# A layer norm's factors, worked out for four token tiles at once, in the last stage of a Fourier, expert and SoLU kernel

## The chip, the cores and the metric

The kernel runs on one core of a Trainium2 chip. The metric is device time in microseconds (us). Before the change three runs took 2077.13, 2080.64 and 2082.59 us; the median is 2080.64. The engines of a core are named PE (TensorE, matrix products), DVE (VectorE), ACT (ScalarE), POOL (GpSimd) and SP (SyncE, which here issues the transfers).

## The reference, cut to what matters

The reference is a chain of three parts: a two-dimensional Fourier transform of 8 x 3072 x 256 numbers, a layer of eight experts in which each of the 24,576 tokens goes to one expert at most, and a gated layer with a layer norm. The change lies in the third:

```
h = x @ w_in                          # 256 -> 1024
e = exp(h - max(h))
sm = e / (sum(e) + 1e-9)
solu = h * sm
mu, var = mean(solu), mean((solu - mu) ** 2)
ln = (solu - mu) / sqrt(var + 1e-6) * g_ln
out = ln @ w_out                      # 1024 -> 256
```

Everything is per token (a row). A layer norm takes out any factor of its row, except that the small 1e-6 has to be scaled with it. The kernel uses that: it never divides by sum(e). It forms u = c * h * e, with some factor c for the row, multiplies u by the weights (the mean is taken out of the weights beforehand), and scales the row of the result by a factor worked out from the sum of e, the variance of u, and c.

## The kernel before, in words

The program runs the Fourier stage, the experts, and then the last stage, which takes the second half of the span. The last stage works on 192 tiles of 128 tokens. Its order is written out by hand: a short list of steps for the first six tiles (`FILL`), and then a loop in which step t does the following, each engine taking its own instructions in this order.

- `mm1(t)`: twelve products on PE give `h` in PSUM, 128 tokens by 1024 (L989). Three buffers of `h`.
- `softmax(t)`: VectorE takes the negative maximum of the row (L999) and scales it (L1000). L1002 makes a power of two out of the maximum's exponent. POOL bounds it (L1003) and multiplies it by the token's input scale (L1004): that is c, one number per token. ScalarE takes the exponential, with the row's sum (L1007).
- `xsplit(t + 7)`: the inputs come in groups of four tiles. With the group's first tile VectorE takes the largest absolute value and makes four small columns of scales `v` (L925 to L929), and POOL multiplies the inputs by one of them (L934); with the second ScalarE rounds them to 16 bits (L945); with the third POOL takes the remainder (L947). The step that has a group's first tile is a step t with t = 1 modulo 4.
- `solu(t - 1)`: VectorE forms u = h * c * e with its sum (L1015). This is the last reader of `h`. ScalarE rounds u to 16 bits (L1018) and takes the sum of squares around the mean (L1020).
- `split(t - 2)`: VectorE takes the remainder (L1026), SP issues a transpose of both halves (L1029), and POOL works out the row's factor in six small instructions of one column (L1031 to L1036; L1035 is the power of -0.5).
- `mm2(t - 5)`: 24 products on PE (L1044 to L1046) into `po`, of which there are two buffers; ScalarE scales the rows by the factor and frees `po` (L1049); the result goes out through SP (L1055) for even tiles, and through a POOL transfer with a list of rows (L1058) for odd ones.

The small per-token columns of a tile lie in `s`, ten columns, with eight buffers. `half` holds -0.5 for the power; `gi`, `wgi` and `wgs` are scales of the weights.

Of the kernel before, what the change touches and what calls it, by code (L numbers as in the profile page):

```python
# [7 lines left out]
FP32 = mybir.dt.float32  # L8
# [3 lines left out]
I32 = mybir.dt.int32  # L12
U32 = mybir.dt.uint32
ACTF = mybir.ActivationFunctionType
ALU = mybir.AluOpType
# [7 lines left out]
F = 1024  # L23
# [26 lines left out]
HEAD_AT = 8  # L50
LAGS = [(2, 4, 5, 2)] * 5 + [(2, 3, 4, 4)] * 2 + [(2, 3, 4, 12)]
WARM = 18
STEPS = [[6, 6]] * 8


@with_exitstack
def kernel(
# [25 lines left out]
    nc = tc.nc  # L83
# [6 lines left out]
    keep = ctx.enter_context(tc.tile_pool(name="keep", bufs=1))  # L90
# [3 lines left out]
    gi = keep.tile([128, 1], FP32, name="gi")  # L94
    gsi = keep.tile([128, 1], FP32, name="gsi")
    wgi = keep.tile([128, 1], FP32, name="wgi")
    wgs = keep.tile([128, 1], FP32, name="wgs")
    half = keep.tile([128, 1], FP32, name="half")
    sc1 = keep.tile([128, 2, E], FP32, name="sc1")
    sc2 = keep.tile([128, 2, E], FP32, name="sc2")  # L100
    ke = keep.tile([128, E], FP32, name="ke")
# [5 lines left out]
    def pow2(dst, src, floor, factor):  # L107
        nc.vector.tensor_scalar(out=dst.bitcast(I32), in0=src.bitcast(I32), scalar1=0x7F800000, scalar2=None, op0=ALU.bitwise_and)
        nc.vector.tensor_scalar(out=dst, in0=dst, scalar1=floor, scalar2=factor, op0=ALU.max, op1=ALU.mult)
# [101 lines left out]
    with ExitStack() as fctx:  # L211
# [128 lines left out]
        groups = [0]  # L340
# [196 lines left out]
        warm = ps2.tile([128, 2, 147], FP32, name="s2")  # L537
        for _ in range(WARM):
            nc.tensor.matmul(warm.rearrange("p a b -> p (a b)"), junk[:, 0:128], junk[:, 0:294], start=True, stop=True)
# [59 lines left out]
        for b in range(B):  # L599
# [15 lines left out]
            ends, k = {}, 0  # L615
            for n in STEPS[b]:
                ends[k + n - 1] = (k, n)
# [264 lines left out]
    with ExitStack() as sctx:  # L882
        XB = 4
        NT = N // 128
        FIRST_X = [1, 1, 2, 2, 2]
        groups = FIRST_X + [XB] * ((NT - sum(FIRST_X)) // XB)
        where = [(g, i) for g, n in enumerate(groups) for i in range(n)]
# [12 lines left out]
        stp = sctx.enter_context(tc.tile_pool(name="sst", bufs=8))  # L900
        op = sctx.enter_context(tc.tile_pool(name="so", bufs=3))
        psh = sctx.enter_context(tc.tile_pool(name="psh2", bufs=3, space=PSUM))
        pso = sctx.enter_context(tc.tile_pool(name="pso", bufs=2, space=PSUM))
        st = {}
        odd = vp.tile([128, B * 12], I32, name="odd", bufs=1)
        nc.sync.dma_start(out=odd, in_=c_out)

        def own_out(r, mine, others):
# [13 lines left out]
        def xscale(g):  # L922
            n = groups[g]
            v = vp.tile([128, 4, XB], FP32, name="v")[:, :, 0:n]
            nc.vector.tensor_reduce(out=v[:, 0], in_=st["x", g], axis=AX.X, op=ALU.max, apply_absolute_value=True)  # L925
            pow2(v[:, 0], v[:, 0], 2.0 ** -100, 0.25)
            nc.vector.reciprocal(v[:, 1], v[:, 0])
            nc.vector.tensor_scalar(out=v[:, 2], in0=v[:, 0], scalar1=wgi, scalar2=None, op0=ALU.mult)
            nc.vector.tensor_scalar(out=v[:, 3], in0=v[:, 0], scalar1=wgi, scalar2=2.0 ** 12, op0=ALU.mult, op1=ALU.mult)  # L929
            st["v", g] = v  # L930
            st["x16", g] = x16p.tile([128, 2 * XB * D], FP16, name="x16")[:, 0:2 * n * D].rearrange("p (s j d) -> p s j d", s=2, d=D)
            if g >= POOL_X:
                r = v[:, 1].unsqueeze(2).to_broadcast([128, n, D])
                nc.gpsimd.tensor_tensor(out=st["x", g], in0=st["x", g], in1=r, op=ALU.mult)  # L934
# [57 lines left out]
        def softmax(t):  # L992
            if t >= NT:
                return
            (g, i), h = where[t], st["h", t]
            v = st["v", g][:, 2, i:i + 1]
            s = stp.tile([128, 10], FP32, name="s")
            st["s", t] = s
            nc.vector.tensor_reduce(out=s[:, 0:1], in_=h, axis=AX.X, op=ALU.max, negate=True)  # L999
            nc.vector.tensor_scalar(out=s[:, 0:1], in0=s[:, 0:1], scalar1=v, scalar2=None, op0=ALU.mult)  # L1000
            si = s.bitcast(I32)
            nc.vector.tensor_scalar(out=si[:, 1:2], in0=si[:, 0:1], scalar1=0x7F800000, scalar2=0x7F800000, op0=ALU.bitwise_and, op1=ALU.bitwise_xor)  # L1002
            nc.gpsimd.tensor_scalar(out=si[:, 1:2], in0=si[:, 1:2], scalar1=0x40000000, scalar2=None, op0=ALU.min)  # L1003
            nc.gpsimd.tensor_scalar(out=s[:, 8:9], in0=s[:, 1:2], scalar1=st["v", g][:, 3, i:i + 1], scalar2=None, op0=ALU.mult)  # L1004
            e = ep.tile([128, F], FP32, name="e")
            st["e", t] = e
            nc.scalar.activation(out=e, in_=h, func=ACTF.Exp, bias=s[:, 0:1], scale=v, accum_out=s[:, 3:4])  # L1007

        def solu(t):
            if not 0 <= t < NT:  # L1010
                return
            h, e, s = st.pop(("h", t)), st.pop(("e", t)), st["s", t]
            u = up.tile([128, F], FP32, name="u")
            st["u", t] = u
            nc.vector.scalar_tensor_tensor(out=u, in0=h, scalar=s[:, 8:9], in1=e, op0=ALU.mult, op1=ALU.mult, accum_out=s[:, 4:5])  # L1015
            u16 = u16p.tile([128, 2, F], FP16, name="u16")
            st["u16", t] = u16
            nc.scalar.copy(u16[:, 0], u)  # L1018
            j = jp.tile([128, F], BF16, name="j")
            nc.scalar.activation(out=j, in_=u, func=ACTF.Square, bias=s[:, 4:5], scale=-float(F), accum_out=s[:, 5:6])  # L1020

        def split(t):
            if not 0 <= t < NT:
                return
            u, u16, s = st.pop(("u", t)), st.pop(("u16", t)), st["s", t]
            nc.vector.tensor_tensor(out=u16[:, 1], in0=u, in1=u16[:, 0], op=ALU.subtract)  # L1026
            ut = utp.tile([128, 16, 128], FP16, name="ut")
            st["ut", t] = ut
            nc.sync.dma_start_transpose(out=ut, in_=u16.rearrange("p a f -> p (a f)"))  # L1029
            q = s[:, 6:7]  # L1030
            nc.gpsimd.tensor_scalar(out=s[:, 2:3], in0=s[:, 1:2], scalar1=2.0 ** 12, scalar2=None, op0=ALU.mult)  # L1031
            nc.gpsimd.tensor_scalar(out=q, in0=s[:, 3:4], scalar1=1e-9, scalar2=s[:, 2:3], op0=ALU.add, op1=ALU.mult)  # L1032
            nc.gpsimd.tensor_scalar(out=q, in0=q, scalar1=q, scalar2=1e-6, op0=ALU.mult, op1=ALU.mult)  # L1033
            nc.gpsimd.tensor_scalar(out=s[:, 5:6], in0=s[:, 5:6], scalar1=float(F) ** -3, scalar2=q, op0=ALU.mult, op1=ALU.add)  # L1034
            nc.gpsimd.tensor_tensor(out=s[:, 7:8], in0=s[:, 5:6], in1=half, op=ALU.pow)  # L1035
            nc.gpsimd.tensor_scalar(out=s[:, 7:8], in0=s[:, 7:8], scalar1=gi, scalar2=None, op0=ALU.mult)  # L1036

        def mm2(t):
            if not 0 <= t < NT:
                return  # L1040
            ut = st.pop(("ut", t))
            po = pso.tile([128, D], FP32, name="po")
            for k in range(8):
                nc.tensor.matmul(po, ut[:, k], wk["gg"][:, k, 0], start=k == 0, stop=False)  # L1044
                nc.tensor.matmul(po, ut[:, k], wk["gg"][:, k, 1], start=False, stop=False)  # L1045
                nc.tensor.matmul(po, ut[:, 8 + k], wk["gg"][:, k, 0], start=False, stop=k == 7)  # L1046
            s = st.pop(("s", t))
            o = op.tile([128, D], FP32, name="o")
            nc.scalar.activation(out=o, in_=po, func=ACTF.Copy, scale=s[:, 7:8])  # L1049
            b, j = divmod(t // 2, 12)  # L1050
            k1 = 4 * j + 1

            def put(lo, hi, tok, steps):
                dst = bass.AP(tensor=out.tensor, offset=out.offset + (b * S + tok) * D, ap=[[n * D, c] for n, c in steps] + [[1, D]])
                own_out(nc.sync.dma_start(out=dst, in_=o[lo:hi]), "even", ("odd",))  # L1055

            if t % 2:
                r = nc.gpsimd.indirect_dma_start(  # L1058
                    out=out,
                    out_offset=bass.IndirectOffsetOnAxis(ap=odd.bitcast(U32)[:, t // 2:t // 2 + 1], axis=0),  # L1060
                    in_=o,
                    in_offset=None,
                    bounds_check=N - 1,
                    oob_is_err=False,
                )
                own_out(r, "odd", ("even", "odd"))
            elif j < 11:
                put(0, 128, k1, [(1, 4), (96, 32)])
            else:
                put(0, 96, k1, [(1, 3), (96, 32)])  # L1070
                put(96, 112, 0, [(96, 16)])
                put(112, 128, 48, [(96, 16)])

        with tc.manual_schedule():
# [8 lines left out]
            for t in range(FILLED, NT + LAG + 1):  # L1083
# [3 lines left out]
                g = xsplit(t + AHEAD)  # L1087
# [121 lines left out]
```

## Time and profile before

| | |
|---|---|
| time, three runs | 2077.13, 2080.64, 2082.59 us |
| span of the profiled execution | 2072.3 us |
| time of the profiled execution | not given beside its span |
| granted TensorE clock, mean over the span | 0.983 |
| busy share of the span | PE 92%, PEld 70%, DVE 79%, ACT 70%, POOL 71% |
| chain that ended last, largest shares | POOL 35%, issue 13%, ACT 3%, DVE 2% |
| first and last start of L989 (the last stage) | 971.6 and 2040.6 us |

The profile is one execution of the program; its times count from the start of its span. "Busy" is the time in which an engine executes; register, branch, semaphore and transfer-issuing instructions don't count. A wait is put down to the instruction whose semaphore came last. Matrix products are pipelined, so the duration of a single one overlaps the next; the distance between starts is what counts. L numbers are lines of the kernel.

### The profile page before, as it was taken

The numbers are of one execution on the slowest core, as the hardware profiler recorded it, in microseconds if no ns is written. First come the engines' busy times: TensorE is split into PE (matmuls) and PEld (weight loads), VectorE is DVE, ScalarE is ACT, GpSimd is POOL, SyncE is SP. The second block draws the span as 40 slices with busy tenths as digits, with TensorE's granted clock in tenths as the row PEclk, the third lists the DMA queues.
The fourth block names the chain that finished last, engine by engine and source line by source line (L and its number), as shares of the span: only waits on it lengthen the run. The fifth ranks groups of instructions, "written<-read, shape, count | busy, mean of one in ns | idle before, by whom it ended". The sixth has DMA issues, their size and how long they took to land.

```text
span 2072.3 us, 43563 instructions
## 1 busy us (share of the span) xinstructions
PE 1912.2 (92%) x14621; PEld 1448.2 (70%) x14621; DVE 1646.0 (79%) x3426; ACT 1454.8 (70%) x2651; POOL 1463.0 (71%) x2260
## 2 busy tenths in 40 slices
PE   8999998789999999898999998999999999999997
PEld 7888886677878878786566665666666666666665
DVE  4767665688988889896988888888888888888884
ACT  6878875566667766684777776777777777677775
POOL 0455657776664566642888888888888888888886
PEclk9999999999999999999999999999999999999999
DMA  9776888233332333323878877888887788787775
GB/s 269 200 204 179 231 247 214 34 94 83 75 80 68 74 77 87 70 68 65 173 160 173 163 158 154 176 157 160 173 164 158 166 169 160 159 174 157 158 157 120
DMA packets 678311, 300.82 MB, mean 145 GB/s; under 512 B 580707, under 2 KB 658155, under 8 KB 678085
## 3 DMA queue, kind: packets, MB, share of 16 engines
q1 hardware_dynamic: 656981, 259.15, 58.4%
q0 software_dynamic: 20992, 38.84, 6.7%
q8 instruction: 115, 1.88, 0.4%
q14 instruction: 111, 0.91, 0.1%
q10 hardware_dynamic: 112, 0.04, 0.0%
HBM read 93.90 MB, written 65.95 MB: 77 GB/s over the span
## 4 chain that ended last, share of the span: by engine, by line
POOL 35%; issue 13%; ACT 3%; DVE 2%; PE 0%; POOLq 0%; DMA 0%; SPq 0%; ACTq 0%
POOL s L1031 5%; POOL out L1058 5%; POOL x L947 5%; POOL sx_sb L934 4%; POOL s L1035 4%; ACT j L1020 3%; POOL s L1004 3%; POOL s L1003 2%; POOL s L1032 2%; POOL s L1033 2%; POOL s L1034 2%; POOL s L1036 2%; DVE u L1015 1%; DVE s L999 0%; DVE u L1026 0%
## 5 line engine op out<-in xcount | busy, mean ns | idle before, releaser
L989 PE MATMUL h<-wi,xT 128*128 128x512 f16 x2304 | 530.5, 380 | 38.1 <-DVE u L1015 31.0
L1044 PE MATMUL po<-gg,ut 128*128 128x256 f16 x1536 | 419.2, 273 | 33.3 <-ACT o L1049 29.1
L989 PEld LDWEIGHTS <-xT 128*128 128x128 f16 x2304 | 221.3, 98 | 285.0 <-DVE u L1015 41.7
L1046 PE MATMUL po<-gg,ut 128*128 128x256 f16 x1536 | 419.2, 273 | 0.0
L1045 PE MATMUL po<-gg,ut 128*128 128x256 f16 x1536 | 419.2, 273 | 0.0
L1015 DVE SCALAR_TENSOR_TENSOR u<-h,s,e 128x1024 f32<-128x1024 f32 x192 | 246.2, 1282 | 164.2 <-POOL s L1004 164.1
L1018 ACT CAST u<-u 128x1024 f16<-128x1024 f32 x192 | 200.4, 1044 | 198.0 <-DVE u L1015 197.9
L453 POOL DMA_INDIRECT tab<-ent,r_ids x192 | 201.0, 1047 | 172.2 <-DMA xs<-t 67.7
L1026 DVE TENSOR_TENSOR u<-u,u 128x1024 f16<-128x1024 f32 x192 | 287.5, 1498 | 0.1
L1007 ACT ACTIVATE e<-h,s,v 128x1024 f32<-128x1024 f32 x192 | 230.4, 1200 | 45.0 <-DVE s L1000 36.6
L792 PE MATMUL py<-w2c,ht 128*128 128x256 f16 x832 | 229.1, 275 | 21.9 <-DVE ht L780 21.9
L773 PE MATMUL ph<-xT,w1c 128*128 128x256 f16 x832 | 227.6, 274 | 17.8 <-DMA xT<-x 13.8
L790 PE MATMUL py<-w2c,ht 128*128 128x256 f16 x832 | 229.1, 275 | 9.9 <-ACT ht L779 8.4
L999 DVE TENSOR_REDUCE s<-h 128x1 f32<-128x1024 f32 x192 | 232.7, 1212 | 0.7 <-PE h L989 0.7
L791 PE MATMUL py<-w2c,ht 128*128 128x256 f16 x832 | 228.9, 275 | 0.5 <-DVE w2c L192 0.5
L774 PE MATMUL ph<-xT,w1c 128*128 128x256 f16 x832 | 227.5, 273 | 0.0
L775 PE MATMUL ph<-xT,w1c 128*128 128x256 f16 x832 | 227.5, 273 | 0.0
L1020 ACT ACTIVATE j<-u,s 128x1024 bf16<-128x1024 f32 x192 | 219.7, 1144 | 0.0
L1045 PEld LDWEIGHTS <-ut 128*128 128x128 f16 x1536 | 150.4, 98 | 71.8 <-issue 39.2
L192 DVE SCALAR_TENSOR_TENSOR w2c<-w_all,ax,w2c 128x512 f16<-128x512 f16 x208 | 166.5, 849 | 26.9 <-ACT w2c L191 26.5
L191 ACT ACTIVATE w2c<-w_all,ax 128x512 f16 x208 | 142.5, 717 | 58.4 <-PE py L792 39.3
L1044 PEld LDWEIGHTS <-ut 128*128 128x128 f16 x1536 | 150.4, 98 | 44.5 <-DMA ut<-u 7.6
(204 smaller groups left out, 4337.1 us busy)
## 6 DMA issues: line engine op xcount, KB each, us to landing
sx_sb<-xs SPq DMA_DIRECT2D x46, 512.0 KB
xt<-x SPq DMA_DIRECT2D x59, 384.0 KB
xs<-t SPq DMA_DIRECT2D x176, 128.0 KB
w_all<-w SPq DMA_DIRECT2D x21, 1024.0 KB
out<-o SPq DMA_DIRECT2D x88, 128.0 KB
tab<-ent,r_ids POOLq DMA_INDIRECT x192
ut<-u SPq DMA_TRANSPOSE x192
d_raw<-w_out SPq DMA_DIRECT2D x8, 256.0 KB
```

What stands on the lines that cost most here:

```text
L790: nc.tensor.matmul(ps[:, h], hh, w[:, 0, k], start=f == 0 and h == 0, stop=False)
L791: nc.tensor.matmul(ps[:, h], hh, w[:, 1, k], start=False, stop=False)
L792: nc.tensor.matmul(ps[:, h], hl, w[:, 0, k], start=False, stop=f == 7 and h == 1)
L989: nc.tensor.matmul(h[:, n * 512:(n + 1) * 512], xT[:, a, c], w, start=c == 0 and k == 0, stop=c == 1 and k == 2)
L999: nc.vector.tensor_reduce(out=s[:, 0:1], in_=h, axis=AX.X, op=ALU.max, negate=True)
L1007: nc.scalar.activation(out=e, in_=h, func=ACTF.Exp, bias=s[:, 0:1], scale=v, accum_out=s[:, 3:4])
L1015: nc.vector.scalar_tensor_tensor(out=u, in0=h, scalar=s[:, 8:9], in1=e, op0=ALU.mult, op1=ALU.mult, accum_out=s[:, 4:5])
L1020: nc.scalar.activation(out=j, in_=u, func=ACTF.Square, bias=s[:, 4:5], scale=-float(F), accum_out=s[:, 5:6])
L1026: nc.vector.tensor_tensor(out=u16[:, 1], in0=u, in1=u16[:, 0], op=ALU.subtract)
L1044: nc.tensor.matmul(po, ut[:, k], wk["gg"][:, k, 0], start=k == 0, stop=False)
L1045: nc.tensor.matmul(po, ut[:, k], wk["gg"][:, k, 1], start=False, stop=False)
L1046: nc.tensor.matmul(po, ut[:, 8 + k], wk["gg"][:, k, 0], start=False, stop=k == 7)
```

## The change

The factor c becomes a constant, 2 to the power of -6. The power of two per token, its two POOL instructions and its VectorE instruction go. The sums of e and of squares of the tiles of a group are gathered in columns of a tile `q` of their own (three rows of four columns). The factors of the rows are worked out once per group, behind `split` of its last tile, by seven POOL instructions on as many columns as the group has tiles (the first groups have 1, 1, 2, 2 and 2 tiles, all others 4). One column of `v` now holds a different value, made from the reciprocal of the input scale, bounded above.

```diff
+U_SCALE = 2.0 ** -6
...
-    half = keep.tile([128, 1], FP32, name="half")
+    half = keep.tile([128, 4], FP32, name="half")
+    wgk = keep.tile([128, 1], FP32, name="wgk")
...
+        nc.vector.tensor_scalar(out=wgk, in0=wgs, scalar1=U_SCALE * 1e-3, scalar2=None, op0=ALU.mult)
...
-            nc.vector.tensor_scalar(out=v[:, 3], in0=v[:, 0], scalar1=wgi, scalar2=2.0 ** 12, op0=ALU.mult, op1=ALU.mult)
+            nc.vector.tensor_scalar(out=v[:, 3], in0=v[:, 1], scalar1=wgk, scalar2=2.0 ** 50, op0=ALU.mult, op1=ALU.min)
             st["v", g] = v
+            st["q", g] = stp.tile([128, 3, XB], FP32, name="q")
...
-            s = stp.tile([128, 10], FP32, name="s")
+            s = stp.tile([128, 2], FP32, name="s")
...
-            si = s.bitcast(I32)
-            nc.vector.tensor_scalar(out=si[:, 1:2], in0=si[:, 0:1], scalar1=0x7F800000, scalar2=0x7F800000, op0=ALU.bitwise_and, op1=ALU.bitwise_xor)
-            nc.gpsimd.tensor_scalar(out=si[:, 1:2], in0=si[:, 1:2], scalar1=0x40000000, scalar2=None, op0=ALU.min)
-            nc.gpsimd.tensor_scalar(out=s[:, 8:9], in0=s[:, 1:2], scalar1=st["v", g][:, 3, i:i + 1], scalar2=None, op0=ALU.mult)
...
-            nc.scalar.activation(out=e, in_=h, func=ACTF.Exp, bias=s[:, 0:1], scale=v, accum_out=s[:, 3:4])
+            nc.scalar.activation(out=e, in_=h, func=ACTF.Exp, bias=s[:, 0:1], scale=v, accum_out=st["q", g][:, 0, i:i + 1])
...
-            nc.vector.scalar_tensor_tensor(out=u, in0=h, scalar=s[:, 8:9], in1=e, op0=ALU.mult, op1=ALU.mult, accum_out=s[:, 4:5])
+            nc.vector.scalar_tensor_tensor(out=u, in0=h, scalar=U_SCALE, in1=e, op0=ALU.mult, op1=ALU.mult, accum_out=s[:, 1:2])
...
-            nc.scalar.activation(out=j, in_=u, func=ACTF.Square, bias=s[:, 4:5], scale=-float(F), accum_out=s[:, 5:6])
+            nc.scalar.activation(out=j, in_=u, func=ACTF.Square, bias=s[:, 1:2], scale=-float(F), accum_out=st["q", g][:, 1, i:i + 1])
...
-            q = s[:, 6:7]
-            nc.gpsimd.tensor_scalar(out=s[:, 2:3], in0=s[:, 1:2], scalar1=2.0 ** 12, scalar2=None, op0=ALU.mult)
-            nc.gpsimd.tensor_scalar(out=q, in0=s[:, 3:4], scalar1=1e-9, scalar2=s[:, 2:3], op0=ALU.add, op1=ALU.mult)
-            nc.gpsimd.tensor_scalar(out=q, in0=q, scalar1=q, scalar2=1e-6, op0=ALU.mult, op1=ALU.mult)
-            nc.gpsimd.tensor_scalar(out=s[:, 5:6], in0=s[:, 5:6], scalar1=float(F) ** -3, scalar2=q, op0=ALU.mult, op1=ALU.add)
-            nc.gpsimd.tensor_tensor(out=s[:, 7:8], in0=s[:, 5:6], in1=half, op=ALU.pow)
-            nc.gpsimd.tensor_scalar(out=s[:, 7:8], in0=s[:, 7:8], scalar1=gi, scalar2=None, op0=ALU.mult)
+            if i == groups[g] - 1:
+                gains(g)
+
+        def gains(g):
+            n = groups[g]
+            q, v = st["q", g], st["v", g]
+            k, r = q[:, 0, 0:n], q[:, 2, 0:n]
+            nc.gpsimd.tensor_scalar(out=k, in0=k, scalar1=1e-9, scalar2=None, op0=ALU.add)
+            nc.gpsimd.tensor_tensor(out=k, in0=k, in1=v[:, 3], op=ALU.mult)
+            nc.gpsimd.tensor_tensor(out=k, in0=k, in1=k, op=ALU.mult)
+            nc.gpsimd.tensor_scalar(out=r, in0=q[:, 1, 0:n], scalar1=float(F) ** -3, scalar2=None, op0=ALU.mult)
+            nc.gpsimd.tensor_tensor(out=r, in0=r, in1=k, op=ALU.add)
+            nc.gpsimd.tensor_tensor(out=r, in0=r, in1=half[:, 0:n], op=ALU.pow)
+            nc.gpsimd.tensor_scalar(out=r, in0=r, scalar1=gi, scalar2=None, op0=ALU.mult)
...
-            nc.scalar.activation(out=o, in_=po, func=ACTF.Copy, scale=s[:, 7:8])
+            nc.scalar.activation(out=o, in_=po, func=ACTF.Copy, scale=st["q", g][:, 2, i:i + 1])
```

## Rows read from the trace of the kernel before

**Rows 1.** Waits of the last stage: who for whom, us, times, longest.
```profile
DVE u L1015 <- POOL s L1004: 164.1, 137, 3.1
...
PE h L989 <- DVE u L1015: 31.0, 45, 1.4
```

**Rows 2.** Stretches: length, busy PE, PEld, DVE, ACT, POOL, clock, DMA, GB/s.
```profile
1015.50:1062.40 46.90, 46.90 (x326) 31.71 (x324) 39.15 (x63) 35.75 (x57) 39.82 (x74) 1.00 0.83 166
...
1480.00:1502.55 22.55, 21.18 (x147) 13.98 (x145) 18.72 (x31) 16.20 (x25) 19.11 (x37) 1.00 0.78 164
```

**Rows 3.** Timeline of PE: start, length, first products of five tiles.
```profile
1015.51 2.75 PE L989 MATMUL h<-wi,xT 128*128 128x512 f16 x12
...
1062.40 2.75 PE L989 MATMUL h<-wi,xT 128*128 128x512 f16 x12
...
1503.52 2.75 PE L989 MATMUL h<-wi,xT 128*128 128x512 f16 x12
...
1526.07 2.75 PE L989 MATMUL h<-wi,xT 128*128 128x512 f16 x12
...
2038.26 2.11 PE L989 MATMUL h<-wi,xT 128*128 128x512 f16 x9
```

**Rows 4.** The stretch from 1480, POOL's instructions on `s` alone: length, busy.
```profile
1480.00:1502.55 22.55, 12.96 (x32) 1.00 0.78 164
```

**Rows 5.** Groups of POOL instructions by shape, last stage: busy, mean ns.
```profile
L1035 POOL TENSOR_TENSOR s<-s,half 128x1 f32<-128x1 f32 x192 | 155.0, 807 | 16.0
...
L934 POOL TENSOR_TENSOR sx_sb<-sx_sb,v 128x1024 f32<-128x1024 f32 x46 | 86.9, 1889 | 0.1
...
L934 POOL TENSOR_TENSOR sx_sb<-sx_sb,v 128x512 f32<-128x512 f32 x2 | 2.1, 1052 | 0.6 <-DVE v L927 0.6
```

**Rows 6.** Timeline, VectorE and POOL, from 1070 to 1076.
```profile
1070.92 1.89 POOL L934 TENSOR_TENSOR sx_sb<-sx_sb,v 128x1024 f32<-128x1024 f32 x1
1070.99 1.28 DVE L1015 SCALAR_TENSOR_TENSOR u<-h,s,e 128x1024 f32<-128x1024 f32 x1 [0.61 <-POOL s L1004]
...
1072.20 1.69 DVE L1026 TENSOR_TENSOR u<-u,u 128x1024 f16<-128x1024 f32 x1
...
1072.90 1.07 POOL L1031 TENSOR_SCALAR s<-s 128x1 f32<-128x1 f32 x1
...
1073.81 1.21 DVE L999 TENSOR_REDUCE s<-h 128x1 f32<-128x1024 f32 x1
...
1074.08 0.27 POOL L1032 TENSOR_SCALAR s<-s 128x1 f32<-128x1 f32 x1
...
1075.06 0.21 DVE L1000 TENSOR_SCALAR s<-s,v 128x1 f32<-128x1 f32 x1
1075.16 0.57 POOL L1035 TENSOR_TENSOR s<-s,half 128x1 f32<-128x1 f32 x1
```

**Rows 7.** Timeline, VectorE's scales of a group of inputs, from 1064.
```profile
1064.32 0.15 DVE L1002 TENSOR_SCALAR s<-s 128x1 int32<-128x1 int32 x1
1064.39 1.21 DVE L925 TENSOR_REDUCE v<-sx_sb 128x4 f32<-128x1024 f32 x1
...
1066.06 0.18 DVE L927 RECIPROCAL v<-v 128x4 f32<-128x4 f32 x1
```

**Rows 8.** Timeline, a subtraction on VectorE and the power on POOL, from 1032.
```profile
1032.97 1.23 DVE L1026 TENSOR_TENSOR u<-u,u 128x1024 f16<-128x1024 f32 x1
...
1033.21 1.42 POOL L1035 TENSOR_TENSOR s<-s,half 128x1 f32<-128x1 f32 x1
```

**Rows 9.** Timeline, the output scaling and the product behind it, from 1506.
```profile
1506.45 0.45 ACT L1049 ACTIVATE o<-po,s 128x256 f32<-128x256 f32 x1
...
1506.95 0.27 PE L1044 MATMUL po<-gg,ut 128*128 128x256 f16 x1 [0.68 <-ACT o L1049]
```

**Rows 10.** Timeline, the last tile's gated product, from 2049.
```profile
2049.71 1.28 DVE L1015 SCALAR_TENSOR_TENSOR u<-h,s,e 128x1024 f32<-128x1024 f32 x1 [3.14 <-POOL s L1004]
```

More of the change, by code (lines that the diff above doesn't have):

```diff
@@ L1011, in solu @@
                 return
-            h, e, s = st.pop(("h", t)), st.pop(("e", t)), st["s", t]
+            g, i = where[t]
+            h, e, s = st.pop(("h", t)), st.pop(("e", t)), st.pop(("s", t))
             u = up.tile([128, F], FP32, name="u")
             st["u", t] = u
-            nc.vector.scalar_tensor_tensor(out=u, in0=h, scalar=s[:, 8:9], in1=e, op0=ALU.mult, op1=ALU.mult, accum_out=s[:, 4:5])
+            nc.vector.scalar_tensor_tensor(out=u, in0=h, scalar=U_SCALE, in1=e, op0=ALU.mult, op1=ALU.mult, accum_out=s[:, 1:2])
             u16 = u16p.tile([128, 2, F], FP16, name="u16")
@@ L1024, in split @@
                 return
-            u, u16, s = st.pop(("u", t)), st.pop(("u16", t)), st["s", t]
+            g, i = where[t]
+            u, u16 = st.pop(("u", t)), st.pop(("u16", t))
             nc.vector.tensor_tensor(out=u16[:, 1], in0=u, in1=u16[:, 0], op=ALU.subtract)
@@ L1046, in mm2 @@
                 nc.tensor.matmul(po, ut[:, 8 + k], wk["gg"][:, k, 0], start=False, stop=k == 7)
-            s = st.pop(("s", t))
+            g, i = where[t]
             o = op.tile([128, D], FP32, name="o")
-            nc.scalar.activation(out=o, in_=po, func=ACTF.Copy, scale=s[:, 7:8])
+            nc.scalar.activation(out=o, in_=po, func=ACTF.Copy, scale=st["q", g][:, 2, i:i + 1])
             b, j = divmod(t // 2, 12)
```

## The prediction, made before the changed kernel ran

> **What bounds the kernel now.** I read four views in this order: the waits of the last stage, busy time by stretch, TensorE's (PE) timeline, and GpSimd's (POOL) own rows. The waits come first. VectorE's gated product (L1015) stood 164.1 us in 137 places because POOL had not finished L1004, and PE stood 31.0 us behind that product, since it frees the PSUM buffer of `h` [rows 1]. Then the stretches. From 1480 a period of four tiles lasts 22.55 us: POOL is busy 19.11 of it, PE 21.18, VectorE 18.72 and ScalarE 16.20. From 1015.5 to 1062.4 PE is busy without a break, with the same work on every other engine and the 16 DMA engines at 0.83 [rows 2]. So two paces can be seen. Nine tiles start between 1015.51 and 1062.40, that is 5.21 us a tile or 20.84 per four: this is PE with nothing in its way. Later, from 1503.52 to 1526.07, four tiles take 22.55 [rows 3]. The stage begins at PE's pace while POOL falls behind, and then runs at POOL's. From tile 9 (1015.51) to tile 191 (2038.26) 182 tiles take 1022.75 us [rows 3], 5.62 each.
>
> **What is removed.** Of POOL's 19.11 us per four tiles, 12.96 in 32 instructions are the eight small ones per token tile on `s` [rows 4]. All 32 go. VectorE loses L1002 per tile (0.15) [rows 7], and the product no longer waits for POOL: it needs only the exponential, which ScalarE finished a step earlier. Seven small POOL instructions per group of four come instead, four columns wide. With the gaps of 0.1 they are 3.5 to 5 us, so POOL falls from 19.1 busy to 10 or 11 and is no longer the bound. VectorE's 18.7 becomes about 18 and ScalarE's 16.2 stays, both under PE's 20.84; [rows 2] show PE's pace held for nine tiles with that work on them. The new constant `wgk` is one VectorE instruction, once. The two changed instructions per group (v, 4 wide) are the same kind as before: nothing. Scaling by a constant in place of a column may shorten L1015 by some 0.05 (L1000 takes 0.21 with a column, L1002 0.15 without) [rows 6, 7]; I count 0, as PE does not wait for it.
>
> **What is added: a wait with a place.** The factors of a group are worked out behind the split of its last tile. In that same step PE's second product for the group's first tile ends, and ScalarE's output scaling (L1049) of that tile now needs them. Behind L1049 on ScalarE stand the next exponential and the input cast; PE waits for L1049 two products later, as `po` has two buffers. I lay the step out from P, the start of its first product on PE.
>
> - `h` is there at P+2.8 (the group of twelve takes 2.75) [rows 3]. VectorE's maximum and scaling take 1.25 [rows 6], the next independent instruction follows in about 0.1, and the scale of the next group of inputs, which falls in this step, takes 1.85 from L925 to the end of L927 [rows 7]. POOL's L934 starts then and takes 1.89 [rows 6]. It ends at E = P+7.95.
> - VectorE's subtraction (L1026) holds POOL off: behind L934 the first small instruction took 1.07 where its neighbours take 0.27 [rows 6]. So the first factor instruction ends at E+1.16, the second starts at E+1.27. The four in the middle step by 0.36 (1074.08 to 1075.16 is three steps) [rows 6]: the power starts at E+2.71.
> - VectorE's next subtraction: the next maximum starts at E+1.0, 1.25 to the scaling, 0.1, 1.21 for the product [rows 6]: E+3.56.
> - The last factor instruction has to start before that. With a power of 0.57, as at one column [rows 5], it starts at E+3.38 and slips through, and L1049 can run at E+3.75. With a power of 0.75 or more it meets the subtraction and waits for it: a power that started 0.24 into a subtraction took 1.42 in place of 0.57, held until 1.09 behind its start [rows 8]. Then the factors are done at E+3.56+1.09+0.30 = E+4.95, L1049 starts at E+5.0, and PE can go on 0.5 later (1506.45 to 1506.95) [rows 9]: E+5.5 = P+13.45.
> - PE wants that buffer at P + 2 x 5.21 + 2.6 (the first product's twelve) = P+13.02. So PE stands still for 0 in the first case and 0.43 per four tiles in the second.
>
> What the power costs at four columns no row shows. From below it is 0.57, no cost per column. From above it is what exceeds an ordinary instruction (0.57 less 0.27) [rows 5, 6] paid four times, 0.27 + 4 x 0.30 = 1.47; below 0.57 is excluded, since three columns more cannot be cheaper. The other instructions get no dearer: L934 goes from 1052 to 1889 ns for 512 elements more, 1.6 ns an element, so three more cost 5 ns [rows 5]. I take 0.9: software that needs 0.30 for one column will need part of that for each further one. Anything between 0.75 and 1.0 gives the same stall, as the subtraction then sets it; at 1.47 the power itself holds the subtraction back, to about E+4.05, and all that follows comes 0.5 later: a stall of 0.9.
>
> The Trainium skill (GPSIMD Engine Reference, Elementwise — side-by-side cycle accounting) counts some 12 cycles of its 1.2 GHz per element for code that branches on its data and less for plain loops. By that three columns more are an estimated 0.03 us, the power is 0.60, and the sum would be the first case, 2003; no run here shows it.
>
> **Sum.** Period 20.84 + 0.43 = 21.27, and 182 tiles are 45.5 of them: 967.8 in place of 1022.75, that is -55.0. At the end of the kernel the last product waited 3.14 for POOL [rows 10]; that goes, but the last three output scalings now wait for the whole last group's factors, about 1: -2. At the start fewer POOL instructions stand ahead of the input's subtraction: -1, between 0 and -3. Together -58. The span of the profiled execution, 2072.3, becomes 2014; its own time is not given beside its span, and the shown runs lie 4.8 to 10.3 above that span (median 8.3), which I leave as it is. 2080.64 - 58 = **2022**.
>
> **Rivals.**
> - *PE's pace in full.* The last factor instruction slips through: 45.5 x 20.84 = 948.2, -74.5, with start and end -77.5: 2003. For it: [rows 2] show 47 us without a stall, with the DMA engines at 0.83. Against it: a margin of 0.2 us only, and a power of 0.75 is enough to lose it.
> - *The slow power.* 1.0 to 1.47: stall 0.5 to 0.9, period 21.3 to 21.75, -53 to -33 with the -3 of the ends: 2026 to 2045.
> - *Slower, by the same wait.* If each POOL instruction pays per column, ScalarE's L1049 and behind it PE stand until the factors come. The whole gain of 22.55 - 20.84 = 1.71 is gone where PE gets the buffer at P+14.7, so with factors done later than E+6.2; at four times the time for each (four of 1.1, a power of 2.3, a last one of 1.2, and a subtraction or two between) they end at about E+10, a stall near 5.5 and a period of 26.4: some +170, 2250. A mild form, factors at E+6.7, is a period of 23.0, +25 less 3: 2102. Against it: the slope of L934.
> - *Transposes late.* The same transfers in 20.84 in place of 22.55 put the DMA engines from 0.78 to about 0.85. If PE then waits 0.4 per four tiles, the first rival becomes 2021. The stretch from 1015.5, with 0.83, speaks against it, but only over nine tiles [rows 2].
> - *It does nothing.* If something else than POOL sets the 22.55, the time stays. The hold of VectorE behind L1004 leaves little room for this.
>
> **How the numbers follow.** The forecast (stall 0.3 to 0.6, 2016 to 2030) gets 0.40; PE's pace 0.30; the slow power 0.15; late transposes 0.03; no change 0.05; slower 0.07. The range 1998 to 2050 holds the first four with a few us on either side for head, end and the median's own spread; it leaves out the last two. Within 0.3% (6.2 us, about what a measurement of this kernel can tell from no change) is 0.05, slower 0.07, faster 0.88.
>
> **What would show it.** In the profile after: the wait of L1015 for POOL gone; POOL busy near half; mm1 starts 20.84 apart per four where I am too low on the gain, 21.2 to 21.4 where I am right; a wait of PE for L1049 in one step of four, and of L1049 for the last factor instruction on POOL, at the step where L934 runs; that last instruction at 1.1 to 1.4 in place of 0.30. The power's own duration at four columns decides between the cases: under 0.7 the first rival, over 1.0 the second. It would be wrong if PE waited for transposes in each period, or if L1015 found another wait.

## The result: 2020.49 us, and where the 59 us came from

| | before | changed |
|---|---|---|
| median of four runs in one comparison | 2081.61 us (2077.13 to 2083.07) | 2020.49 us (2015.09 to 2027.64) |
| span of the profiled execution | 2072.3 us | 2013.1 us (its own time 2015.09) |
| tile 9 to tile 191, starts of the first product | 1022.75 us | 969.67 us |
| usual period of four tiles | 22.55 us | 21.33 us |

The ratio is 0.9715 [0.9691, 0.9739]: faster, and 2022 was forecast. The spans differ by 59.2 us. Of that 53.1 lie between tile 9 and tile 191 of the last stage, 4.2 between tile 0 and tile 9 (43.92 against 39.75), 3.7 behind the start of the last tile's products (34.0 against 30.3); everything before the stage took 1.8 longer (its first product starts at 973.35).

The waits of the last stage, changed kernel, from 960 on: engine, what waits, what it waits for, us in total, times, longest.

```profile
POOL out L1067 <- ACT o L1058: 430.3, 91, 9.3
ACT o L1058 <- POOL q L1045: 150.1, 46, 4.3
DVE s L1003 <- PE h L993: 141.0, 136, 1.5
...
PE po L1053 <- ACT o L1058: 14.7, 44, 0.9
...
DVE u L1016 <- ACT e L1007: 0.5, 1, 0.5
```

The two waits of [rows 1] are gone: the gated product (now L1016) waited once, 0.5 us, and that for ScalarE. VectorE now waits for TensorE (L1003 for `h`, 141.0 us in 136 places), which is how the stage looks when TensorE sets the pace. In their place is the wait that was forecast: ScalarE's output scaling L1058 waits for the last factor instruction L1045 in 46 places, once per group, and TensorE stands 14.7 us in 44 of them (0.33 on average, counted from the modelled end of the product before; by the distance between starts, below, each place costs 0.48). POOL's largest sum (L1067, the odd outputs) costs nothing, as POOL has time to spare.

One period of four tiles, and the stretch of [rows 2] again (busy us and instructions of PE, PEld, DVE, ACT, POOL; then clock, DMA share, GB/s), changed kernel:

```profile
1503.70:1525.03 21.33, 21.00 (x147) 14.10 (x145) 17.41 (x27) 15.78 (x26) 10.51 (x12) 1.00 0.97 171
1015.50:1062.40 46.90, 46.57 (x323) 31.47 (x322) 40.18 (x64) 36.31 (x58) 22.38 (x24) 1.00 0.96 181
```

POOL is busy 10.51 of 21.33 us where it had 19.11 of 22.55. The DMA engines show a share of 0.97, and TensorE does not wait for them.

TensorE's first products in that period, changed kernel (start, duration, engine, line):

```profile
1503.70 2.75 PE L993 MATMUL h<-wi,xT 128*128 128x512 f16 x12
...
1508.91 2.75 PE L993 MATMUL h<-wi,xT 128*128 128x512 f16 x12
...
1514.12 2.75 PE L993 MATMUL h<-wi,xT 128*128 128x512 f16 x12
...
1519.81 2.75 PE L993 MATMUL h<-wi,xT 128*128 128x512 f16 x12
```

Two tiles 5.21 apart, then one of 5.69: the 0.48 us lost per period lie in one place. Here is that place, POOL and VectorE side by side (start, duration, engine, line, operation; in brackets the idle time before it and its releaser):

```profile
1509.80 1.93 POOL L938 TENSOR_TENSOR sx_sb<-sx_sb,v 128x1024 f32<-128x1024 f32 x1 [0.89 <-DVE v L930]
...
1511.03 1.78 DVE L1028 TENSOR_TENSOR u<-u,u 128x1024 f16<-128x1024 f32 x1
...
1511.80 1.10 POOL L1039 TENSOR_SCALAR q<-q 128x4 f32<-128x4 f32 x1
...
1512.98 0.20 POOL L1040 TENSOR_TENSOR q<-q,v 128x4 f32<-128x4 f32 x1
...
1513.98 0.21 DVE L1004 TENSOR_SCALAR s<-s,v 128x1 f32<-128x1 f32 x1
1514.11 1.22 DVE L1016 SCALAR_TENSOR_TENSOR u<-h,e 128x1024 f32<-128x1024 f32 x1
1514.12 1.04 POOL L1044 TENSOR_TENSOR q<-q,half 128x4 f32<-128x4 f32 x1
...
1515.25 1.22 DVE L1028 TENSOR_TENSOR u<-u,u 128x1024 f16<-128x1024 f32 x1
1515.27 1.37 POOL L1045 TENSOR_SCALAR q<-q,gi 128x4 f32<-128x4 f32 x1
...
1516.67 0.47 ACT L1058 ACTIVATE o<-po,q 128x256 f32<-128x256 f32 x1 [3.34 <-POOL q L1045]
...
1517.20 0.27 PE L1053 MATMUL po<-gg,ut 128*128 128x256 f16 x1 [0.33 <-ACT o L1058]
```

The reader is to see 1515.25 and 1515.27. The last factor instruction L1045 starts 0.02 us behind VectorE's subtraction L1028 and takes 1.37 us, until the subtraction is over; where it meets nothing it takes 0.30 (below). L1058 follows at once, TensorE 0.53 later.

### The profile page after: what moved, and what is told of

Same layout as the page of the kernel before. It is cut to its first block, busy times and chain, and to the rows that moved or that the text cites. A ratio compares the mean times of both kernels' runs of the same rounds, so it can differ in the third digit from the quotient of the medians.

```text
span 2013.1 us, 41918 instructions
## 1 busy us (share of the span) xinstructions
PE 1905.9 (95%) x14621; PEld 1456.8 (72%) x14621; DVE 1586.3 (79%) x3235; ACT 1435.9 (71%) x2651; POOL 1053.1 (52%) x1081
## 4 chain that ended last, share of the span: by engine, by line
PE 25%; POOL 14%; DVE 7%; issue 3%; ACT 1%; DMA 1%; POOLq 0%; ACTq 0%
PE h L993 12%; PE po L1053 4%; POOL sx_sb L938 4%; PE po L1055 4%; PE po L1054 4%; POOL q L1045 3%; DVE s L1003 3%; DVE v L928 3%; POOL q L1039 2%; POOL q L1044 2%; ACT o L1058 1%; POOL q L1042 1%; POOL q L1043 1%; POOL q L1040 0%; POOL q L1041 0%
## 5 line engine op out<-in xcount | busy, mean ns | idle before, releaser
L1053 PE MATMUL po<-gg,ut 128*128 128x256 f16 x1536 | 418.5, 272 | 16.7 <-ACT o L1058 14.7
L1003 DVE TENSOR_REDUCE s<-h 128x1 f32<-128x1024 f32 x192 | 234.5, 1221 | 141.0 <-PE h L993 141.0
L1067 POOL DMA_INDIRECT out<-o,odd x96 | 101.3, 1055 | 447.8 <-ACT o L1058 430.3
L1028 DVE TENSOR_TENSOR u<-u,u 128x1024 f16<-128x1024 f32 x192 | 262.9, 1369 | 27.8 <-ACT u L1019 27.8
L1016 DVE SCALAR_TENSOR_TENSOR u<-h,e 128x1024 f32<-128x1024 f32 x192 | 233.8, 1218 | 0.6 <-ACT e L1007 0.5
L1058 ACT ACTIVATE o<-po,q 128x256 f32<-128x256 f32 x192 | 90.1, 470 | 155.1 <-POOL q L1045 150.1
L1054 PEld LDWEIGHTS <-ut 128*128 128x128 f16 x1536 | 150.2, 98 | 59.1 <-issue 27.0
```

What stands on the lines that cost most here:

```text
L1016: nc.vector.scalar_tensor_tensor(out=u, in0=h, scalar=U_SCALE, in1=e, op0=ALU.mult, op1=ALU.mult, accum_out=s[:, 1:2])
```

## The experiments

Theory A, that of the forecast: POOL's queue set 22.55; now TensorE sets the pace, less a stall of about 0.48 per period, which exists only because L1045 comes just behind the subtraction. Rivals: the power L1044 itself holds the subtraction back (B); part of the loss is transfers or something else at TensorE's pace (C). These runs were on other chips, whose first two stages take some 150 us longer at a lower granted clock (0.87 to 0.90 on average up to 1110 us, against 0.97 up to 970 us in the first trace of the changed kernel; in the last stage it is 1.00 in all traces). So ratios are compared, and the last stage by itself: the changed kernel's tiles 9 to 191 take 969.67, 964.09 and 969.17 us on three chips.

| kernel | tiles 9 to 191, us | usual period | ratio to before |
|---|---|---|---|
| factors earlier | 948.22 | 20.84 | 0.9648 [0.9615, 0.9681] |
| constant alone | 948.22 | 20.84 | 0.9661 [0.9621, 0.9702] |
| batch alone | 948.48 | 20.84 | 0.9665 [0.9622, 0.9708] |
| product for power | 948.22 | 20.84 | one run |
| changed, again | 964.09 | 21.32, some 20.84 | 0.9704 [0.9665, 0.9743] |
| small instruction added | 948.22 | 20.84 | 0.9631 [0.9597, 0.9665] |
| power twice | 990.96 | 22.43 and 21.37 in turn | one run |
| before, product for power | 960.72 | 21.24, first ones 20.84 | one run |
| factors earlier, again | 948.22 | 20.84 | 0.9622 [0.9584, 0.966] |
| changed beside it | 969.17 | 21.33 | 0.9727 [0.9686, 0.9768] |

The first four rows shared one chip, the next four another, the last two a third.

**Factors earlier.** The seven instructions are issued ahead of the input scaling L938 of the same step.

```diff
         def split(t):
...
-            if i == groups[g] - 1:
-                gains(g)
...
                 softmax(t)
+                gains(t - 2)
                 g = xsplit(t + AHEAD)
```

> The same seven factor instructions per group, but queued on GpSimd ahead of the scaling of the next inputs instead of behind it, in the same step. Theory (the stall of TensorE behind the output scaling comes from the place of the factors in GpSimd's queue, behind that 1.93 us instruction): the factors are done about 3 us earlier, the wait of the output scaling for them goes, four tiles take 20.84 instead of 21.33, and the time falls by 45.5 x 0.49 = 22, to about 1998 (ratio to the kernel before 0.960). Rival (the 21.33 is something else, transposes or VectorE's backlog): the period stays at 21.3 and the time at 2020 (0.9715).

Its timeline at the same place:

```profile
1513.29 0.24 POOL L1039 TENSOR_SCALAR q<-q 128x4 f32<-128x4 f32 x1
...
1514.74 1.05 POOL L1044 TENSOR_TENSOR q<-q,half 128x4 f32<-128x4 f32 x1
...
1515.90 0.30 POOL L1045 TENSOR_SCALAR q<-q,gi 128x4 f32<-128x4 f32 x1
1516.17 1.89 POOL L938 TENSOR_TENSOR sx_sb<-sx_sb,v 128x1024 f32<-128x1024 f32 x1
...
1516.42 2.72 DVE L1028 TENSOR_TENSOR u<-u,u 128x1024 f16<-128x1024 f32 x1
```

and its waits for the factors from 1240 on, of which one place is left, with one period, busy by engine as above:

```profile
ACT o L1058 <- POOL q L1045: 0.3, 1, 0.3
...
1500.00:1520.84 20.84, 20.84 (x146) 14.10 (x145) 18.12 (x27) 15.88 (x26) 9.21 (x11) 1.00 0.98 176
```

The stage falls by 21 us to 45.5 x 20.84 = 948.2, and TensorE is busy without a break. This is what theory A says (B is settled by the power twice, below), and C falls: at TensorE's pace nothing else is late, with the DMA engines at 0.98. The ratio is 0.9648 and not 0.960, as the kernel before takes 2243.55 us on this chip: a saving of some 81 us in all (59 and 22) leaves 0.964 of that. The price is visible too: the subtraction now stands behind the long L938 and takes 2.72 in place of 1.22, which delays nothing.

**The constant alone.** Factors per tile as before, without the power of two.

```diff
-            if i == groups[g] - 1:
-                gains(g)
+            gains(g, i)
...
-            nc.gpsimd.tensor_tensor(out=r, in0=r, in1=half[:, 0:n], op=ALU.pow)
+            nc.gpsimd.tensor_tensor(out=r, in0=r, in1=half[:, 0:1], op=ALU.pow)
```

> One part alone: the constant in place of the power of two per token, but the factors still worked out per tile, seven one-column instructions on GpSimd for each tile. Theory (before, GpSimd's queue set 22.55 per four tiles; a cut of more than 1.71 is enough to hand the bound to TensorE): eight instructions of 0.25 to 0.29 with their gaps go, some 2.8 us per four tiles, one more of 0.2 per tile comes, about 1.2; so GpSimd needs some 20.5 to 21 and TensorE's 20.84 or little more is reached: period 20.9 to 21.3, time 2000 to 2020. And the output scaling has no long wait, as the factors of a tile are due three steps later. Rival (the factors for four tiles at once are what gains): less than a third of the gain, 2060 or above.

One period of this kernel, busy by engine as above:

```profile
1500.00:1520.84 20.84, 20.84 (x146) 14.08 (x145) 18.36 (x26) 15.78 (x26) 17.12 (x33) 1.00 0.87 177
```

POOL is busy 17.12 of 20.84 and TensorE never stops. This part alone takes the stage to TensorE's pace, though with little to spare: 17.46 busy, in the kernel before with a product for the power (below), are too much.

**The batch alone.** Factors for four tiles at once, the power of two per token kept (VectorE's instruction and two on POOL per tile).

```diff
+            nc.vector.tensor_scalar(out=c.bitcast(I32), in0=s.bitcast(I32)[:, 0:1], scalar1=0x7F800000, scalar2=0x7F800000, op0=ALU.bitwise_and, op1=ALU.bitwise_xor)
+            nc.gpsimd.tensor_scalar(out=c.bitcast(I32), in0=c.bitcast(I32), scalar1=0x40000000, scalar2=None, op0=ALU.min)
+            nc.gpsimd.tensor_scalar(out=s[:, 2:3], in0=c, scalar1=st["v", g][:, 3, i:i + 1], scalar2=None, op0=ALU.mult)
...
-            nc.vector.scalar_tensor_tensor(out=u, in0=h, scalar=U_SCALE, in1=e, op0=ALU.mult, op1=ALU.mult, accum_out=s[:, 1:2])
+            nc.vector.scalar_tensor_tensor(out=u, in0=h, scalar=s[:, 2:3], in1=e, op0=ALU.mult, op1=ALU.mult, accum_out=s[:, 1:2])
```

> The other part alone: factors for four tiles at once, with the power of two per token and its two GpSimd instructions and one VectorE instruction kept. Theory: GpSimd is relieved of some 9 us per four tiles and no longer the bound; the same stall as in the changed kernel behind the output scaling stays, and the product's wait for GpSimd comes back only in the step in which the factors run, with two steps to spare: period 21.3 to 21.6, time 2018 to 2035. Rival (the product's wait for the two instructions is itself what cost the time): period above 22, time above 2055.

A miss. Its timeline (here L1049 is the last factor instruction, L1032 the subtraction, L1006 the power of two on VectorE):

```profile
1503.53 1.05 POOL L1048 TENSOR_TENSOR q<-q,half 128x4 f32<-128x4 f32 x1
1503.67 0.15 DVE L1006 TENSOR_SCALAR q<-s 128x1 int32<-128x1 int32 x1
1503.75 1.28 DVE L1020 SCALAR_TENSOR_TENSOR u<-h,s,e 128x1024 f32<-128x1024 f32 x1
1504.68 0.31 POOL L1049 TENSOR_SCALAR q<-q,gi 128x4 f32<-128x4 f32 x1
...
1504.96 1.27 DVE L1032 TENSOR_TENSOR u<-u,u 128x1024 f16<-128x1024 f32 x1
```

The last factor instruction starts 0.28 ahead of the subtraction and takes 0.31. VectorE has one small instruction more in front of the product, which starts 0.33 behind the maximum's scaling (1503.42) in place of 0.13, and the product takes 1.28 in place of 1.22: the subtraction comes some 0.26 later and the meeting does not happen. From 1140 on the product waits for POOL nowhere, so the rival falls as well. So either part alone, on the chip where both were run, reaches 20.84; together, on three other chips, they reach 21.33.

**A product for the power.** The power's place in the queue stays, its length goes.

```diff
-            nc.gpsimd.tensor_tensor(out=r, in0=r, in1=half[:, 0:n], op=ALU.pow)
+            nc.gpsimd.tensor_tensor(out=r, in0=r, in1=half[:, 0:n], op=ALU.mult)
```

> The changed kernel with the power of the factors replaced by a product on the same four columns, so the rows of the output carry another factor than the reference's. Theory (the power, 1.04 us at four columns, makes the last factor instruction miss the start of VectorE's subtraction, and it then waits for the whole of that): at about 0.2 us it is 0.8 earlier, the last instruction takes 0.3 in place of 1.3, TensorE's wait goes and the period is 20.84. Rival (the wait comes from the length of the chain and not from that meeting): the last instruction keeps its 1.3, the period falls by at most a little.

By shape, from 1240 on:

```profile
L1045 POOL TENSOR_SCALAR q<-q,gi 128x4 f32<-128x4 f32 x41 | 12.1, 295 | 4.2
L1044 POOL TENSOR_TENSOR q<-q,half 128x4 f32<-128x4 f32 x41 | 8.2, 199 | 3.2
```

With 0.199 us in L1044's place, L1045 slips through (0.295) and the stall is gone.

**The changed kernel again, and one small instruction added.** The second kernel puts one more 128x1 instruction per tile on VectorE, between the maximum's scaling and the product; nothing reads its result.

```diff
+            nc.vector.tensor_scalar(out=s[:, 2:3], in0=s[:, 0:1], scalar1=1.0, scalar2=None, op0=ALU.mult)
```

> The changed kernel as it is, beside the others of this call, since the first four ran on another chip than it did. Theory: the last stage depends on no chip, so its period is 21.3 per four tiles again, with TensorE's wait behind the output scaling in each. Rival (the first four reached 20.84 because of their chip): 20.84 here too.

> The changed kernel with one useless VectorE instruction more per tile, one column, where the power of two was made before (about 0.15 us, 0.25 with its wait for the scaling ahead of it). Theory (in the changed kernel the last factor instruction becomes ready 0.02 us behind the start of VectorE's subtraction and then waits for all of it; in the run of the batch alone it was 0.28 ahead, since VectorE did 0.3 more per tile): the subtraction starts some 0.1 to 0.25 later, the last factor instruction takes 0.3 in place of 1.3, and the period falls to 20.84, so that with an instruction more the kernel is 22 us faster (1%). Rival (the batch alone reached 20.84 for another reason, such as its waits for GpSimd): the period stays at 21.3 or grows by the instruction.

The place in the kernel with the added instruction (L1005; the lines behind it are one further down):

```profile
1500.70 0.15 DVE L1005 TENSOR_SCALAR s<-s 128x1 f32<-128x1 f32 x1
1500.77 1.22 DVE L1017 SCALAR_TENSOR_TENSOR u<-h,e 128x1024 f32<-128x1024 f32 x1
1501.73 0.30 POOL L1046 TENSOR_SCALAR q<-q,gi 128x4 f32<-128x4 f32 x1
...
1501.91 1.22 DVE L1029 TENSOR_TENSOR u<-u,u 128x1024 f16<-128x1024 f32 x1
```

The margin goes from 0.02 behind to 0.18 ahead, by the 0.19 that the product starts later (0.32 behind the maximum's scaling in place of 0.13), and the kernel with more work is the faster one: 2152.44 against 2165.11 us on the same chip (six runs each, 2142.92 to 2157.78 and 2152.86 to 2174.35, which overlap), the stage 948.22 against 964.09. That is less than the 22 us expected, since the changed kernel did not stall in every period: it ran 12 of its 45 periods at 20.84 here. In ten of those VectorE is late by another meeting,

```profile
1316.76 1.97 DVE L932 TENSOR_SCALAR v<-v,wgk 128x4 f32<-128x4 f32 x1
1316.82 1.88 POOL L938 TENSOR_TENSOR sx_sb<-sx_sb,v 128x1024 f32<-128x1024 f32 x1 [1.50 <-DVE v L930]
```

L932, a 0.23 us instruction elsewhere, takes until POOL's L938 is over; the product and both subtractions move back, and L1045 gets through in 0.30. No count of busy time would have shown that more work is faster.

**The power twice.** The changed kernel with the power worked out a second time.

```diff
+            nc.gpsimd.tensor_tensor(out=q[:, 3, 0:n], in0=r, in1=half[:, 0:n], op=ALU.pow)
```

> The changed kernel with the power done twice, the first time into a column that nobody reads. Theory (GpSimd and VectorE hold each other off, whole instructions): the second power starts just ahead of the subtraction, holds it to its own end, and the last factor instruction comes behind both: about 0.97 later than now, TensorE's wait grows from 0.49 to 1.45 and the period to 22.3. Rival (VectorE does not wait for a GpSimd instruction of four columns): the subtraction starts on time, and the factors are late by 0.1 to 0.3 only, period 21.4 to 21.6.

Both answers came, in turn. In the periods of 21.37 (24 of 45) the second power (L1045 here) starts 0.02 ahead of the subtraction,

```profile
1514.31 1.01 POOL L1045 TENSOR_TENSOR q<-q,half 128x4 f32<-128x4 f32 x1
...
1514.33 1.26 DVE L1028 TENSOR_TENSOR u<-u,u 128x1024 f16<-128x1024 f32 x1
1515.43 0.33 POOL L1046 TENSOR_SCALAR q<-q,gi 128x4 f32<-128x4 f32 x1
```

and the subtraction takes 1.26, not 2.2: a power under way does not hold VectorE, which ends B. In the periods of 22.43 (18 of 45) both start within the same 0.01 us, the power waits for all of the subtraction, and the last factor instruction follows that:

```profile
1491.89 2.10 POOL L1045 TENSOR_TENSOR q<-q,half 128x4 f32<-128x4 f32 x1
...
1491.89 1.22 DVE L1028 TENSOR_TENSOR u<-u,u 128x1024 f16<-128x1024 f32 x1
...
1494.09 0.30 POOL L1046 TENSOR_SCALAR q<-q,gi 128x4 f32<-128x4 f32 x1
```

The trace of the kernel before agrees with more than 0.02 us between the two: 43 times a subtraction starts 0.37 us behind a one-column power, and both take their usual time, as here:

```profile
1067.22 0.57 POOL L1035 TENSOR_TENSOR s<-s,half 128x1 f32<-128x1 f32 x1
...
1067.59 1.22 DVE L1026 TENSOR_TENSOR u<-u,u 128x1024 f16<-128x1024 f32 x1
```

**The kernel before with a product for the power.** The queue of POOL becomes shorter by about 0.37 us a tile (0.57 less 0.20); everything else stays.

```diff
-            nc.gpsimd.tensor_tensor(out=s[:, 7:8], in0=s[:, 5:6], in1=half, op=ALU.pow)
+            nc.gpsimd.tensor_tensor(out=s[:, 7:8], in0=s[:, 5:6], in1=half, op=ALU.mult)
```

> The kernel before with its one-column power replaced by a product, so the rows of the output carry another factor than the reference's. Theory (GpSimd's queue set the 22.55): 0.36 less per tile, 1.4 per four tiles, or a little less where the wait for VectorE's subtraction only moves to another instruction: a period of 20.9 to 21.6. Rival (the latency from the maximum to the scaled factor, L1002 to L1004, set it, not the queue's length): the period stays above 22.

The period falls from 22.55 to 21.24, and tiles 9 to 191 take 960.72 in place of 1022.75 us. One such period, busy by engine as above, and the first wait of [rows 1], from 1140 on:

```profile
1600.00:1621.24 21.24, 21.03 (x147) 14.01 (x144) 18.69 (x31) 16.21 (x25) 17.46 (x37) 1.00 0.84 174
...
DVE u L1015 <- POOL s L1004: 67.9, 66, 1.5
```

POOL is busy 1.65 less per period (17.46 for 19.11; the power's place took 0.81 us on average with its waits and now takes 0.40), and the period is 1.31 shorter. The edit is on POOL alone, so the length of POOL's queue did set the 22.55. The constant alone, with 17.12 busy, has no such wait; but it also makes the product independent of POOL, so beside this run it does not show which of the two matters. The batch alone does: there the product still needs POOL's two instructions, POOL is busy 13.39 of 20.84, and the product does not wait for it.

**Factors earlier and the changed kernel, side by side.**

> The factors queued ahead of the scaling of the inputs once more, now in one call with the changed kernel, as a version that should beat it. Theory: the last stage is 45.5 periods of 20.84 in place of about 21.3, 16 to 22 less, which is 0.7 to 1.1% of either time. Rival (what the stage gives is lost at its ends, since the inputs are scaled 3 us later): less than 0.3% between the two.

> The changed kernel for that comparison. Theory: periods of 21.32, with some of 20.84 among them, and a ratio to the kernel before near 0.971. Rival: no period of 21.32.

2141.39 us (ratio 0.9622 [0.9584, 0.966]) against 2168.73 (0.9727 [0.9686, 0.9768]): the version with the factors earlier beats both kernels. No run of the first (2130.49 to 2152.98) is as slow as any of the second (2154.00 to 2175.13). The stage explains 21 of the 27 us. The other 6 are less than the runs of one kernel differ among themselves, and the two traces already differ by 17.6 us where the last stage starts (1110.81 and 1128.40), ahead of all that the edit touches.

## Why the prediction was right

- **The bound.** "No longer the bound" held: POOL 10.51 us busy of a period (10 to 11 forecast), L1016's wait for it gone, and the before kernel's reaction to a shorter queue shows that POOL set its pace.
- **The place of the stall.** TensorE waits for L1058 and L1058 for L1045, in the step of L938, once per group, as laid out. L938 ends at P + 8.03 (7.95 forecast), L1045 takes 1.37 (1.1 to 1.4), TensorE goes on 0.48 late (0.43), the period is 21.33 (21.27). Tiles 9 to 191 gave 53.1 us of the 55.0.
- **It was closer than the forecast made it.** Two terms were off in opposite directions. The four instructions in the middle step by 0.29, not 0.36 (L1040 starts at 1512.98, the power at 1514.12), so the power began 0.32 earlier than said, at E + 2.39. And the power takes 1.04, not 0.9. With the real steps a power of 0.9 would have ended early enough for L1045 to start at about E + 3.40, ahead of the subtraction at E + 3.52: TensorE's pace in full, 21 us less. So the point that decides lay near 1.0 for the power, not at 0.75, and the forecast's own 0.9 would have been on the other side of it. That the stall came at all, and with it the 2022, is in part luck: two errors of opposite sign left the forecast on the right side of that point. The size of the stall is not luck: once L1045 meets the subtraction, the subtraction sets it, and that was laid out at E + 3.56. The chances of 0.40 and 0.30 for the two cases say fairly that this was open.
- **The slow power.** At 1.04 the power lies in this rival's range, and by the forecast's own sign (over 1.0) its time of 2026 to 2045 us should have come; 2020.49 came. The mechanism given for the longer stall is refuted by the doubled power: a power that is already running does not hold the subtraction back. POOL waits for VectorE here.
- **The Trainium skill's prices.** The estimate of 0.60 for four columns, from the Trainium skill's figure (GPSIMD Engine Reference, Elementwise — side-by-side cycle accounting), is not borne out: 1.04 was measured. The Trainium skill (SBUF — State Buffer, Who interferes with whom) says that a VectorE instruction with two inputs in SBUF contends with a GpSimd instruction that reads SBUF, that the pair of ports they share is an exclusive lock, and that the order of issue decides who is blocked. The traces agree for L1045 behind the subtraction (1.37 against 0.30) and for the subtraction behind L938 (1.78 against 1.22); they differ for the subtraction 0.02 behind a 1.01 us power, which took 1.26, and for those 0.37 behind a one-column power, which took 1.22.
- **What was priced at nothing.** The forecast laid out the subtraction without L1002, in the right place (E + 3.52 against 3.56), but did not see that L1002's going is what brings the meeting about: the kernels with one small instruction more there have their subtraction some 0.2 us later and no stall. The 0.06 that the product gains by its constant (1.28 to 1.22), counted as 0 because TensorE does not wait for it, works the same way, where the margin is 0.02.
- **Start and end.** -4.2 and -3.7 where -1 and -2 were taken. At the end the last product started without a wait and the last odd output was issued 21.9 us behind the start of the last tile's products in place of 25.6; for the start no run separates the causes.
- **Rivals that fell.** Late transposes: a DMA share of 0.98 at 20.84 without a stall (about 0.85 was forecast from the pace; the share rose by more, and TensorE did not wait). No change, and slower: the gain is there, and the small POOL instructions cost the same at four columns as at one (L1041: 199 and 195 ns). The mild form of "slower" was also summed too high: a period of 23.0 is 45.5 x 0.45 = 20 us more, not 25. Nothing else hangs on that.

## What to carry to other kernels

Once a queue stops being the bound, look at where the small, late-needed instruction stands in it: put instructions whose inputs are ready early ahead of a long one, and ahead of the meeting with another engine, as the version with the factors earlier does for 1.3% on top. Where a layout on paper leaves a margin of one or two tenths of a microsecond, forecast both cases and say which duration decides. And measure the parts of a change alone: in the last stage here each part gave more than the two together (948 us against 964 to 970).

## What was not expected of the hardware

The power's cost by columns, changed kernel, from 960 to 2014 (count, busy us, mean ns of one, idle before):

```profile
L1044 POOL TENSOR_TENSOR q<-q,half 128x4 f32<-128x4 f32 x46 | 48.0, 1042 | 3.6
...
L1044 POOL TENSOR_TENSOR q<-q,half 128x2 f32<-128x2 f32 x3 | 2.2, 722 | 0.2
...
L1044 POOL TENSOR_TENSOR q<-q,half 128x1 f32<-128x1 f32 x2 | 1.2, 592 | 0.2
```

Each further column costs about 0.15 us, while ordinary instructions there cost nothing for it. That 0.02 us decide over 0.48 in each period, and that the same kernel has periods of 21.32 and of 20.84 in one execution, was not expected either; nor that a 128x4 scaling on VectorE (L932) can take 1.97 us beside a long POOL instruction that starts 0.06 behind it, while VectorE's subtraction runs beside a short one that began before it.
